# An attention-and-gating kernel in a fixed order of instructions: the order searched anew with more slack behind its transfers

## The chip, the cores and the metric

The kernel runs on one core of a Trainium2 chip. The metric is the device time of one execution in microseconds (us), lower being better. The core has five engines that run side by side and wait for each other by semaphores only: TensorE (PE, matrix products and transposes), VectorE (DVE), ScalarE (ACT), GpSimd (POOL) and SyncE (SP, which issues transfers). Sixteen DMA engines move data between the memory outside and the two memories on the core: SBUF, and PSUM, into which TensorE writes.

## The reference: chunk-selecting attention, then a gated layer

```python
# attention: q, k, v of shape (4, 8, 768, 64); chunks of 32 keys, 24 of them, 6 kept for each query
k_min = np.min(k_chunks, axis=3)
k_max = np.max(k_chunks, axis=3)
ub = np.sum(np.maximum(q[:, :, :, None, :] * k_min[:, :, None, :, :],
                       q[:, :, :, None, :] * k_max[:, :, None, :, :]), axis=-1)
ub = np.where(causal, ub, -1000000000.0)
top_chunks = np.argsort(ub, axis=-1)[..., -top_k:]
scores = scale * np.matmul(q, k.transpose(0, 1, 3, 2))
...                                           # mask: in a selected chunk, and not in the future
attn = np.exp(scores - np.max(scores, axis=-1, keepdims=True))
attn = attn / (np.sum(attn, axis=-1, keepdims=True) + 1e-09)
x = np.matmul(attn, v)                        # heads side by side: (4, 768, 512)

# gated layer
h = np.maximum(x @ w_in, 0.0)
u, v = (h[..., :d_ff // 2], h[..., d_ff // 2:])
v_n = (v - mu) / np.sqrt(var + 1e-06)         # over the last axis
v_s = np.einsum('ts,bsd->btd', w_spatial, v_n) + b_spatial[None, :, None]
return ((u * v_s) @ w_out).astype(np.float32)
```

## The kernel before

The work is cut into about 1,400 small operations with names. A pair `i` (0 to 15) is two heads of a batch; a batch `b` has four pairs; a group `g` is two pairs, loaded together. The number behind a name is the pair, or the batch and the tile of 128 rows. Names that matter here:

- `lk`, `lq`, `lv`: loads of keys, queries and values, issued by GpSimd; `win`, `wsp`, `wout`, `lb`: loads of the weights.
- `kT`, `kTb`, `qT`: transposes on TensorE; `kmax`, `kmin`, `kb`: bounds of the chunks on VectorE; `ub`: the upper bounds on TensorE; `top`, `sel`: the selection on VectorE; `kop`: copy of the transposed keys into the operand of the scores; `kh`: filling of that operand's constant half; `rq`: the positive and negative parts of the queries.
- `aT`, `ac`: transposes of the query operand and the copy out of PSUM, for pairs 0 to 7; `aTd`: the same as one transposing transfer of SyncE, for pairs 8 to 15.
- `sc`, `ex`, `av`: scores, exponentials, and the product with the values; `tri`: the causal triangle on GpSimd, from pair 4 on; `rc`, `nm`: normalisation on VectorE.
- `x`: transposition of the attention's output (by SyncE from pair 4 to pair 14); `v`, `u`, `s`, `o`: the four matrix products of the gated layer in pieces of two matmuls; `gt`: the gate; `gd`: transposition of the gate (SyncE, but for the last two, which go over TensorE, `gp`, and a copy, `gd`); `oc`, `os`: copy and store of the output.
- `dm`: matmuls on zeros that keep TensorE's clock up before there is work; `ring`, `small`, `expand`, `mlat`, `mtri`: constants.

A table says of each operation which engine has it, what it waits for and which buffers it takes. Each row also has an assumed duration. A search outside the kernel puts the operations into one list by means of these assumptions, and that list is what the kernel emits:

```python
DEF=dict(...,sc=3,tr=1,acc=1,ml=3,...,tm=.8,lm=0.2,lm2=1.2,...)
...
# loads of pair groups 1 to 7: (service time, assumed flight time)
op(f'lk{g}{hi}','POOL',1.007,...,dma=(p['svk'],1.9+(p['lm'] if g<4 else p['lm2'])))
...
# SyncE's transposing transfers: tm is the slack behind each
op(f'aTd{i}','SP',1.44,deps=[f'sel{i}'],acq=[('a',i)],uses=[('qs',g)],prio=pr(20),dma=(2.46,1.5+p['tm']))
...
op(f'x{i}','SP',1.22,deps=[f'nm{i}0',f'nm{i}1'],acq=[('xT',b)],uses=[('x16',i)],prio=t0+18,dma=(1.23,1.5+p['tm']))
...
else: op(f'gd{b}{ti}','SP',1.22,deps=[f'gt{b}{ti}'],acq=[('gT',f'{b}{ti}')],uses=[('g',f'{b}{ti}')],...,dma=(.82,1.5+p['tm']))
...
for n in p['flip']:                     # copies that go to the other of ScalarE and VectorE
    e,oc=o.alts; ...; o.eng,o.occ=e,oc
...
for k in range(p['dum']): op(f'dm{k}','PE',mmc(128),...)
```

```python
PLAN = {..., 'dum': 50, ..., 'flip': [...], 'lm': 0.2, 'lm2': 1.2, 'tm': 0.8, ...}
ORDER = """
dz id0 dm small lk000 ring2 ring1 lk010 ring0 lq000 ring3 id1 lq010 expand lk011 kh01 kh00 kh31 lk001 kT0 kh11 lq011
...
"""
...
with tc.manual_schedule():
    for name in ORDER.split():
        acts[name]()
```

Each engine runs its own operations in the order of the list, one after the other. The assumed durations are used nowhere else: they set no wait in the kernel. The buffers concerned: two for `x16` (the normalised output that `x` reads), three for `g`, one PSUM bank for `acc`, three for `sc`, three for the gated layer, and six for the output.

```python
def normalise(self, hi):                                    # nm
    if not hasattr(self, "x16"):
        self.x16 = sb.tile([P, NQT, 2, D], F16, tag="x16", name="x16")      # the pool has 2
    nc.vector.tensor_tensor(self.x16[:, :, hi, :], in0=self.av[hi][:, :, 0:D], ...)

def x_dma(self):                                            # x
    nc.sync.dma_start_transpose(out=self.x_dest()..., in_=self.x16.rearrange("p t h d -> p (t h d)"))

def gate():                                                 # gt
    g = st["g", ti] = ml.tile([P, DH], F16, tag="g", name="g", bufs=3)
    nc.vector.scalar_tensor_tensor(g, in0=st["s", ti], scalar=b_col[:, ti:ti + 1], in1=st["u"][:, ti, :], ...)

def gate_dma():                                             # gd
    st["gT", ti] = ml.tile([P, KO, P], F16, tag="gT", name="gT", bufs=NQT)
    if (b, ti) in prm["gp"]:
        copier(engine[f"gd{b}{ti}"])(st["gT", ti], st["gp", ti])
        return
    nc.sync.dma_start_transpose(out=st["gT", ti], in_=st["g", ti])

def scores(self, hi, g):                                    # sc
    sc = self.sc[hi, g] = ps_sc.tile([P, 512], F32, tag="sc", name="sc")
    for si, (t, q0, n, col) in enumerate(TILES[g]):
        diag = self.b == 0 and si == 0
        mm(sc[:, col:col + n], lhsT=self.kh[hi][:, t * P:(t + 1) * P], rhs=self.a[:, ...], start=True, stop=not diag)
        if diag:
            mm(sc[:, 0:P], lhsT=identity, rhs=tri, start=False, stop=True)
```

Of the kernel before, what the change touches and what calls it, by code (L numbers as in the profile page):

```python
# [166 lines left out]
def mmc(n): return max(n/2.4+2.5,25)/1000  # L167
DEF=dict(BEATS=12,pa=8,dve_a=(),qx=('ACT',),xp=4,mlp_first=13,mlp_mul=1.0,sc=3,tr=1,acc=1,ml=3,kbuf=3,qbuf=3,vbuf=3,ebuf=3,late=240,chunk=2,
  lk=40,lq=36,lv=18,kdma=99,kcp=2,kcdma=1,kc_act=(),shift=4,prep=0.0,tm=.8,lm=0.2,lm2=1.2,gp=(),head=1,lag=0.0,kp=27,ca=99,tree=0,svk=1.48,rpool=(),ract=(),svh=.96,svw=1.15,flip=(),wide=0,pt=(),kdm=0,xd=(),dum=0,dum0=42,split=1,warm0=0.,qa_dve=(),ma_act=(),mkbuf=2)
PEL=0.2  # L170
def build(prm=None):
    p=dict(DEF); p.update(prm or {})
# [17 lines left out]
    f=0.9  # L190
# [5 lines left out]
    for g in range(1,8):  # L196
        t0=2*g*BE
# [13 lines left out]
    for i in range(NPAIR):  # L211
        b,hp=divmod(i,HP); g,x=divmod(i,2)
        t0=i*BE
# [39 lines left out]
        ca=i>=p['ca']  # L253
# [36 lines left out]
        for hi in range(2):  # L290
            for gg in range(6):
                c=sum(mmc(n) for (_,_,n,_) in TILES[gg])+(mmc(128) if b==0 else 0)
                W_=p['wide']; kk=f'{i}{hi}{gg//2 if W_ else gg}'
                op(f'sc{i}{hi}{gg}','PE',c,PEL,deps=(adep[hi] if not hd else [f'acA0{hi}']+(['acB0'] if gg else []))+[f'kop{i}{hi}',f'kh{i%4}{hi}']+(['mtri'] if b==0 else []),acq=[('sc',kk)],uses=[('a',i),('kh',i)],prio=t0+6*hi+gg)
                if W_ and gg%2==0: continue
                op(f'ex{i}{hi}{gg//2 if W_ else gg}','ACT',(.493 if gg<5 else .16) if not W_ else (.915 if gg<5 else .60),.104,deps=[f'sc{i}{hi}{gg}']+([f'sc{i}{hi}{gg-1}'] if W_ else []),acq=[('e',f'{i}{hi}')],uses=[('sc',kk)],prio=t0+6*hi+gg+.1)
            EX=(lambda r: [f'ex{i}{hi}{gg}' for gg in sorted({x//2 for x in r})]) if p['wide'] else (lambda r: [f'ex{i}{hi}{gg}' for gg in r])
            tri=[]
            if b>0:
                op(f'tri{i}{hi}','POOL',.82,.05,deps=EX(range(6)),uses=[('e',f'{i}{hi}')],prio=t0+6*hi+6); tri=[f'tri{i}{hi}']  # L300
# [90 lines left out]
PLAN = {'late': 40, 'mlp_first': 8, 'qbuf': 5, 'kbuf': 6, 'vbuf': 6, 'dum': 50, 'warm0': 5.3, 'kcp': 99, 'flip': ['ac11', 'ac20', 'ac31', 'ac40', 'ac41', 'ac51', 'ac70', 'ac71', 'kc10', 'kc11', 'kc8', 'kc9', 'kh01', 'kh21', 'kh31', 'kop100', 'kop101', 'kop110', 'kop111', 'kop120', 'kop141', 'kop150', 'kop31', 'kop40', 'kop50', 'kop51', 'kop71', 'kop81', 'kop90', 'kop91', 'oc10', 'oc11', 'oc12', 'oc13', 'oc14', 'oc15'], 'gp': ((3, 4), (3, 5)), 'lm': 0.2, 'lm2': 1.2, 'tm': 0.8, 'dum0': 42, 'split': 1, 'rpool': (4,), 'ract': (1,)}  # L391

ORDER = """
dz id0 dm small lk000 ring2 ring1 lk010 ring0 lq000 ring3 id1 lq010 expand lk011 kh01 kh00 kh31 lk001 kT0 kh11 lq011
dm0 kTb0 kh30 kmin0 dm1 dm2 dm3 dm4 dm5 dm6 lq001 dm7 dm8 dm9 dm10 dm11 kop00 kmax0 qTb0 mlat qT0 dm12 lk10 dm13 rq01
dm14 dm15 dm16 rq00 dm17 dm18 dm19 dm20 dm21 dm22 dm23 kb0 kop01 ub0 lk11 kT1 top00 kTb1 kmin1 lv0 dm24 dm25 dm26 dm27
dm28 kop11 dm29 dm30 dm31 dm32 dm33 dm34 dm35 dm36 dm37 selA0 dm38 kmax1 kop10 aTA00 aTA01 mtri dm39 dm40 dm41 kh10
acA00 qT1 lq10 top01 sc000 kb1 dm42 dm43 sel0 dm44 ex000 rq11 aTB0 lq11 dm45 rq10 kh20 dm46 dm47 dm48 dm49 acB0 ub1
acA01 lb sc001 top10 sc005 kT2 ex001 sc002 win00 top11 ex005 sc004 sel1 ex002 win30 sc013 kmax2 aT10 ex004 lk21 sc010
ex013 sc003 kop21 ex010 lq20 sc011 kop20 aT11 ex003 av000 ex011 kmin2 sc015 lk20 av001 sc012 ac10 av002 ac11 lq21  # L400
ex015 sc100 ex012 rc00 kb2 sc014 kh21 ex100 nm00 qT2 lv1 qT3 ex014 rq21 sc102 sc112 rq20 ex102 kT3 rq30 sc101 win21
ex112 av010 kmin3 ub2 win10 ex101 sc104 sc111 win01 top20 ex104 av011 sc103 kmax3 av012 ex111 sc114 win31 ex103 sc113
top21 ex114 rc01 sc110 kb3 sel2 ex113 sc105 rq31 aT21 lk30 ex110 nm01 aT20 ex105 sc115 kop30 ac21 av100 ub3 ac20 av101
ex115 lk31 kop31 av102 top30 sc200 sc201 rc10 top31 ex200 kT4 nm10 sc205 ex201 win11 sc203 sel3 av110 ex205 kmin4
ex203 sc202 sc204 ex202 qT4 kmax4 av111 ex204 sc215 sc210 av112 ex215 aT30 rq41 ex210 sc213 rc11 rq40 kop40 sc211 wsp5
sc212 kb4 nm11 xp0 lq31 ex213 ub4 kop41 av200 ac30 av201 top40 win20 aT31 ex211 x0 av202 kT5 lq30 ex212 top41 sc214
kop50 sc300 rc20 sel4 sc301 lv2 nm20 qT5 ex214 ac31 av210 ex300 xp1 rq51 sc310 ex301 rq50 wsp0 av211 sc311 kmin5 ex310
aT40 sc303 ex311 av212 kmax5 sc304 ex303 wsp1 sc302 kT6 ex304 rc21 wout3 ac40 sc312 ex302 sc315 nm21 aT41 ex312 x1
sc305 av300 ex315 wsp3 ex305 sc313 kb5 kop51 ac41 sc404 sc314 kmin6 av301 ex313 ub5 av302 ex404 wsp4 top50 sc415 xp2
ex314 rc30 sc401 lk40 top51 ex415 nm30 sc402 ex401 sc403 sel5 ex402 av310 kop60 sc400 ex403 sc405 kT7 lk41 kmax6 ex405  # L410
aT50 ex400 av311 sc412 ac50 av312 kop61 ring4 sc411 ex412 rc31 sc501 x2 qT6 ex411 sc414 nm31 ex501 tri40 sc502 rq61
xp3 ex414 rq60 sc413 av400 wsp2 ex502 kmax7 aT51 ex413 lq40 sc410 sc500 x3 kop71 sc504 kb6 av401 ac51 v00.0 lq41 ex410
av402 kop70 ub6 ex500 sc513 kmin7 v00.2 ex504 lk51 sc503 ex513 sc512 kb7 v04.0 ex503 top60 lv3 v02.0 va00 top61 sc510
rc40 v04.2 sel6 ex510 nm40 sc514 lq50 qT7 ex512 v02.2 rq70 va04 av410 rq71 tri41 v03.0 va02 bs00 sc505 av411 ex514
aT60 bs04 sc511 ex505 av412 ac60 v03.2 lk50 rc41 bs02 v01.0 ex511 sc603 nm41 va03 ub7 tri50 v01.2 ex603 top70 x4 wsT0
lv4 va01 vs00 av500 top71 wsT1 wsc0 sc601 av501 sel7 sc600 ex601 lq51 bs03 sc602 v05.0 ex600 vs02 sc515 aT61 vs04 wsc1
ex602 wout1 sc605 v05.2 bs01 ac61 av502 u00.0 rc50 va05 vs01 u01.0 vs03 nm50 ex515 sc613 ex605 bs05 aT70 tri51 ex613
sc610 kT8 ac70 ex610 sc612 vs05 av510 kmin8 ex612 sc611 u00.2 ex611 kmax8 av511 sc615 qT8 ua00 sc704 av512 ex615 rq81
sc604 u01.2 ex704 rq80 sc703 ex604 rc51 kb8 aT71 nm51 sc700 ex703 sc614 tri60 ac71 av600 rs0 sc702 kop80 av601 ua01
ub8 av602 vn04 ex700 wsT2 rc60 ex614 nm60 sc701 wsT4 ex702 top80 tri61 av610 ex701 sc713 top81 sc712 kop81 av611 lk60  # L420
sel8 sc711 av612 wsc2 qT9 aTd8 ex713 rc61 wsT3 wsc4 wout0 u02.0 ex711 vn02 lv7 sc705 u04.0 ex712 vn00 x5 u02.2 ex705
wsc3 u04.2 ua02 nm61 tri70 sc710 wsT5 ua04 vn01 u03.0 ex710 wsc5 av700 sc715 rq90 sc714 u03.2 vn03 ex714 u05.0 vn05
ex715 kT9 ua03 tri71 u05.2 kmin9 s00.0 ua05 av701 s00.2 kmax9 s01.0 s00.4 rq91 kop90 s01.2 kb9 gt00 ub9 kop91 s01.4
top90 gd00 av702 sc801 top91 sc802 sc805 ex801 s02.0 rc70 sel9 kT10 ex802 gt01 aTd9 sc800 ex805 s02.2 nm70 ex800 sc810
sc815 kmin10 s02.4 ex810 x6 av710 ex815 qT10 kmax10 sc803 av711 sc804 ex803 av712 gt02 s03.0 gd01 ex804 sc814 rc71
kop100 s03.2 nm71 tri80 sc812 kb10 kT11 rq100 x7 kop101 s03.4 wout2 rq101 sc811 ex812 lq60 av800 gt03 ub10 gd02 kop111
s05.0 top100 s04.0 lq61 ex814 top101 s05.2 kmin11 ex811 av801 lq71 sc901 sc813 s05.4 ex901 sel10 sc903 kmax11 ex813
lk61 aTd10 qT11 s04.2 ex903 av802 kop110 sc911 lv5 sc904 rc80 sc914 nm80 s04.4 ex911 gt05 o00.0 ex914 lk70 sc902 kb11
av810 rq110 ex904 v10.0 ex902 tri81 sc913 o00.2 gt04 ex913 sc900 av811 oc00 rq111 sc915 v10.2 gd04 o02.0 va10 av812
sc905 o01.0 ex915 gd03 rc81 ex900 ub11 ex905 v11.0 top110 tri90 o02.2 bs10 v11.2 oc02 o01.2 top111 va11 sc910 v13.0  # L430
oc01 bs11 sc1000 v13.2 sel11 v12.0 nm81 va13 v14.0 ex910 qT12 bs13 kT12 ex1000 v14.2 kmax12 v12.2 va14 av900 vs13
sc912 va12 kop121 sc1002 av901 ex912 aTd11 sc1003 vs10 o03.0 kmin12 ex1002 tri91 sc1012 av902 ex1003 o03.2 rc90 x8
ex1012 lv6 v15.0 nm90 kop120 sc1005 kb12 sc1010 bs14 v15.2 av910 ex1005 bs12 ex1010 lq70 u10.0 gd05 oc03 sc1013 rq121
sc1001 av911 vs11 va15 rq120 lk71 u10.2 ex1013 sc1004 bs15 av912 ex1001 u11.0 rc91 sc1015 nm91 ua10 ub12 sc1014 vs14
ex1004 u11.2 top120 x9 o04.0 top121 ua11 tri100 kT13 vs15 sel12 ex1014 o04.2 kmin13 sc1011 ex1015 av1000 ex1011 sc1104
aTd12 kmax13 av1001 qT13 ex1104 sc1101 tri101 av1002 vs12 sc1112 ex1101 rq130 sc1114 u12.0 rc100 oc04 nm100 sc1102 rs1
u12.2 kop131 ex1112 av1010 o05.0 vn14 ex1114 av1011 kop130 sc1110 ex1102 o05.2 rq131 ua12 sc1100 av1012 kb13 ex1110
# [653 lines left out]
```

The softmax here doesn't subtract the row's maximum and nothing guards it: scores larger than these inputs give would overflow.

## Time and profile before

| what | value |
|---|---|
| time, median of three | 204.93 us (204.6 to 205.82) |
| span of the profiled execution | 202.8 us |
| TensorE, VectorE, ScalarE, GpSimd busy | 191.7, 158.9, 152.7, 80.9 us |
| granted TensorE clock | 1.00 |
| SyncE's transposes, median from issue to landing | gate 2.7, x 3.2, query operand 4.4 us |
| GpSimd's loads of k, q, v, median from issue to landing | 7.6, 7.1, 7.9 us |

A line of a group or of the chain names the engine, the line of the kernel and the tile written; L956 is every matmul of the gated layer, L832 the scores, L858 the product with the values, L868 `nm`, L999 `gt`, L877 `x`, L825 `aTd`, L1014 `gd`. A wait is put down to what came last before it ended. In the chain, a DMA piece runs from the issue to the landing.

### The profile page before, as it was taken

What the parts mean: (1) busy time and instruction counts of PE and PEld (TensorE: products, weight loads), DVE (VectorE), ACT (ScalarE), POOL (GpSimd) and SP (SyncE); (2) the same over time, 40 slices, a digit from 0 to 9 for tenths busy, and PEclk for the clock granted to TensorE, in tenths of its full rate; (3) what the DMA queues carried; (4) which work ended last, traced back from release to release, by engine and by line L of the source; (5) the groups of instructions that cost most, each with busy time, mean ns of one, the idle gap of its engine ahead of it and who ended that gap; (6) DMA issues with size and microseconds to landing.
All of it is one profiled execution on the core that took longest, in us unless ns stands there. A gap on an engine that the chain in (4) does not pass through costs nothing.

```text
span 202.8 us, 5261 instructions
## 1 busy us (share of the span) xinstructions
PE 191.7 (95%) x2043; PEld 121.0 (60%) x2043; DVE 158.9 (78%) x480; ACT 152.7 (75%) x299; POOL 80.9 (40%) x97
## 2 busy tenths in 40 slices
PE   7899899999999999999989999999999999999992
PEld 7776677876677755565456665556556555444441
DVE  6899799999899999796679999797677555367440
ACT  5979799999989976799589986594989542663141
POOL 7999858848871461196145211110113101000000
PEclk9999999999999999999999999999999999999999
DMA  6999999999999099989999958479181349150365
GB/s 39 108 119 165 157 179 170 161 198 133 150 142 157 1 106 116 207 99 151 149 129 181 157 143 157 123 167 181 39 214 61 91 102 122 26 209 0 81 248 192
DMA packets 113482, 27.02 MB, mean 133 GB/s; under 512 B 108465, under 2 KB 110001, under 8 KB 113457
## 3 DMA queue, kind: packets, MB, share of 16 engines
q0 software_dynamic: 76544, 12.20, 83.2%
q1 hardware_dynamic: 36912, 14.49, 36.6%
q8 instruction: 16, 0.26, 0.5%
q14 instruction: 10, 0.07, 0.1%
HBM read 24.38 MB, written 6.29 MB: 151 GB/s over the span
## 4 chain that ended last, share of the span: by engine, by line
PE 56%; DMA 17%; ACT 11%; POOL 6%; DVE 6%; issue 2%; SPq 1%; DVEq 0%; POOLq 0%
PE mlp L956 34%; PE sc L832 11%; ACT e L841 9%; DMA gT<-g 8%; PE acc L858 6%; DMA xT<-x 5%; DMA qs<-in_q_dram 4%; POOL k L618 2%; DVE g L999 1%; ACT kh L739 1%; POOL qs L618 1%; PE trq L744 1%; ACT a L822 1%; PE ub L764 1%; PE kTp L679 1%
## 5 line engine op out<-in xcount | busy, mean ns | idle before, releaser
L841 ACT ACTIVATE e<-sc 128x512 f16<-128x512 f32 (+1 forms) x192 | 92.9, 561 | 14.5 <-PE sc L832 10.9
L832 PE MATMUL sc<-a,kh 128*128 128x512 f16 (+3 forms) x256 | 61.8, 305 | 1.9 <-ACT a L822 0.5
L847 POOL TENSOR_SCALAR_AFFINE_SELECT e<-e 128x768 f16<-128x768 f16 x24 | 21.1, 877 | 80.8 <-ACT e L841 57.1
L956 PE MATMUL mlp<-w_in_sb,xT 128*128 128x512 f16 x192 | 51.9, 378 | 0.0
L858 PEld LDWEIGHTS <-e 128*128 128x128 f16 x672 | 31.5, 97 | 13.8 <-DVE x L868 0.9
L956 PE MATMUL mlp<-vn,wsT 128*128 128x512 f16 x144 | 38.3, 379 | 0.0
L858 PE MATMUL acc<-vt,e 128*128 128x65 f16 x672 | 35.9, 193 | 0.4 <-DVE x L868 0.4
L832 PEld LDWEIGHTS <-kh 128*128 128x128 f16 x256 | 22.6, 97 | 13.7 <-issue 0.7
L703 DVE TENSOR_REDUCE kmm<-kTp 128x24 f16<-128x768 f16 x32 | 29.8, 950 | 1.0 <-PE kTp L679 0.8
L956 PE MATMUL mlp<-w_out_sb,gT 128*128 128x512 f16 x92 | 26.7, 379 | 0.8 <-DMA gT<-g 0.5
L999 DVE SCALAR_TENSOR_TENSOR g<-mlp,b_col,u 128x512 f16<-128x512 f32 x24 | 18.0, 748 | 11.1 <-PE mlp L956 8.6
L956 PEld LDWEIGHTS <-xT 128*128 128x128 f16 x192 | 17.0, 97 | 14.5 <-issue 0.8
L978 DVE BATCH_NORM_STATS2 stats<-vraw 128x6 f32<-128x512 f32 x24 | 16.1, 684 | 9.0 <-ACT vraw L973 9.0
L988 ACT ACTIVATE u<-mlp 128x512 f16<-128x512 f32 x24 | 14.2, 599 | 9.1 <-PE mlp L956 8.4
L1019 ACT COPY o<-mlp 128x512 f32<-128x512 f32 x17 | 9.9, 585 | 13.5 <-PE mlp L956 13.4
L956 PEld LDWEIGHTS <-wsT 128*128 128x128 f16 x144 | 12.6, 97 | 10.7
L868 DVE TENSOR_TENSOR x<-acc,rec 128x384 f16<-128x384 f32 x32 | 17.6, 551 | 1.4 <-DMA xT<-x 1.0
L973 ACT ACTIVATE vraw<-mlp 128x512 f32<-128x512 f32 x24 | 14.0, 610 | 4.4 <-PE mlp L956 4.4
L774 DVE MAX8 max<-ub 128x8 f32<-128x8 f32 (+4 forms) x160 | 15.3, 165 | 1.6 <-PE ub L764 1.3
L603 POOL DMA_DIRECT2D k<-in_k_dram x14 | 14.7, 1047 | 1.5 <-DMA qs<-in_q_dram 1.1
L993 DVE TENSOR_SCALAR vn<-vraw,mv,rstd 128x512 f16<-128x512 f32 x24 | 13.7, 605 | 1.3 <-ACT rstd L1029 1.3
L609 POOL DMA_DIRECT2D qs<-in_q_dram x14 | 14.5, 1042 | 0.2 <-issue 0.2
(81 smaller groups left out, 238.0 us busy)
## 6 DMA issues: line engine op xcount, KB each, us to landing
out_dram<-o SPq DMA_DIRECT2D x23, 256.0 KB, 2.4
vt<-in_v_dram POOLq DMA_DIRECT2D x8, 384.0 KB, 7.9
k<-in_k_dram POOLq DMA_DIRECT2D x14, 192.0 KB, 7.6
qs<-in_q_dram POOLq DMA_DIRECT2D x14, 192.0 KB, 7.1
ws_raw<-in_moe_w_spatial_dram POOLq DMA_DIRECT2D x6, 192.0 KB, 7.8
w_in_sb<-in_moe_w_in_dram POOLq DMA_DIRECT2D x8, 128.0 KB, 7.9
w_out_sb<-in_moe_w_out_dram POOLq DMA_DIRECT2D x4, 128.0 KB, 6.9
k<-in_k_dram POOLq DMA_DIRECT2D x4, 96.0 KB, 3.4
```

The source lines that it names most:

```text
L603: nc.gpsimd.dma_start(out=k_tile(g)[:, :, :, hi, :].rearrange("p x t d -> p (x t) d"), in_=source(k, b, 2 * hp + 2 * hi, 2))
L609: nc.gpsimd.dma_start(out=t.rearrange("p x t d -> p (x t) d"), in_=source(q, b, 2 * hp + 2 * hi, 2))
L703: nc.vector.tensor_reduce(self.kmm[:, m, :], src, axis=AX.X, op=op, negate=(m == 1))
L774: nc.vector.max(self.max8[:, qi - 1, hi, :], self.ub[:, c0:c0 + CPT * (qi + 1)])
L832: mm(sc[:, col:col + n], lhsT=self.kh[hi][:, t * P:(t + 1) * P], rhs=self.a[:, q0 // P:(q0 + n) // P, hi, :], start=True, stop=not diag)
L841: nc.scalar.activation(out=self.e[hi][:, g * 512:g * 512 + width], in_=self.sc[hi, g][:, 0:width], func=Act.Exp, scale=scale)
L847: nc.gpsimd.affine_select(out=blk, in_=blk, compare_op=Alu.is_ge, fill=0.0, base=0, channel_multiplier=-1, pattern=[[0, NQT], [1, P]])
L858: mm(self.av[hi][:, qi, :], lhsT=self.e[hi][:, c:c + P], rhs=self.v[hi][:, t, 0:D + 1], start=first and n == 0, stop=last and n == len(blo ...
L868: nc.vector.tensor_tensor(self.x16[:, :, hi, :], in0=self.av[hi][:, :, 0:D], in1=self.rec[hi].to_broadcast([P, NQT, D]), op=Alu.mult)
L956: mm(st[kind, ti], lhsT=lhsT, rhs=rhs, start=(j == 0), stop=(j == n - 1))
L978: nc.vector.bn_stats(st["stats", ti], st["vraw"][:, ti, :])
L999: nc.vector.scalar_tensor_tensor(g, in0=st["s", ti], scalar=b_col[:, ti:ti + 1], in1=st["u"][:, ti, :], op0=Alu.add, op1=Alu.mult)
```

## The change

Two of the search's assumptions are larger: the slack behind each SyncE transpose, `tm`, goes from 0.8 to 1.6 us, and the slack behind the loads of groups 1 to 3, `lm`, from 0.2 to 0.6 us. It is meant to keep consumers from being listed so close behind a transfer that they wait for it when it lands late. The list of all operations was then searched anew. Seven more zero matmuls are in it (`dum` 50 to 57), and the set of copies that are swapped between ScalarE and VectorE differs. The condition of the diagonal matmuls is written with a parameter that has the same effect.

```diff
-PLAN = {'late': 40, 'mlp_first': 8, 'qbuf': 5, 'kbuf': 6, 'vbuf': 6, 'dum': 50, ..., 'flip': ['ac11', 'ac20', 'ac31', 'ac40', 'ac41', 'ac51', 'ac70', 'ac71', 'kc10', 'kc11', 'kc8', 'kc9', 'kh01', 'kh21', 'kh31', 'kop100', 'kop101', 'kop110', 'kop111', 'kop120', 'kop141', 'kop150', 'kop31', 'kop40', 'kop50', 'kop51', 'kop71', 'kop81', 'kop90', 'kop91', 'oc10', 'oc11', 'oc12', 'oc13', 'oc14', 'oc15'], ..., 'lm': 0.2, 'lm2': 1.2, 'tm': 0.8, ...}
+PLAN = {'late': 40, 'mlp_first': 8, 'qbuf': 5, 'kbuf': 6, 'vbuf': 6, 'dum': 57, ..., 'flip': ['ac10', 'ac11', 'ac21', 'ac31', 'ac40', 'ac41', 'ac51', 'ac60', 'ac71', 'gd34', 'gd35', 'kc10', 'kc11', 'kc8', 'kc9', 'kh00', 'kh01', 'kh31', 'kop100', 'kop101', 'kop111', 'kop140', 'kop141', 'kop150', 'kop31', 'kop40', 'kop50', 'kop51', 'kop71', 'kop81', 'kop90', 'kop91', 'oc05', 'oc10', 'oc12', 'oc14', 'oc15'], ..., 'lm': 0.6, 'lm2': 1.2, 'tm': 1.6, ...}
 ORDER = """
-dz id0 dm small lk000 ring2 ring1 lk010 ring0 lq000 ring3 id1 lq010 expand lk011 kh01 kh00 kh31 lk001 kT0 kh11 lq011
+dz id0 dm ring2 lk000 small lk010 ring3 lq000 id1 lq010 expand lk011 ring0 kh10 lk001 kh00 kT0 kh21 kh01 kh31 lq011
 ... (the whole list; the same names but for dm50 to dm56)
-                diag = self.b == 0 and si == 0
+                diag = self.i < prm["trip"] and si == 0        # trip = 4
```

The order of SyncE's transfers from pair 8's query operand to the gates of batch 0, and of GpSimd's loads in that stretch:

```
SyncE before   x4 aTd8 x5 gd00 aTd9 x6 gd01 x7 gd02 aTd10 gd04 gd03 aTd11 x8 gd05 x9 aTd12 x10
SyncE after    x4 aTd8 x5 x6 gd00 aTd9 gd01 gd02 x7 aTd10 gd03 x8 gd04 aTd11 gd05 aTd12 x9
GpSimd before  lv4 lq51 wout1 lk60 wout0 lv7 wout2 lq60 lq61 lq71 lk61 lv5 lk70 lv6 lq70 lk71
GpSimd after   lq51 lk60 lk50 lv4 lq50 lv7 wout0 wout2 lk61 lq61 lq60 lk71 lv5 lk70 lq70 lq71 lv6
```

## The prediction

> **What bounds the kernel now.** I read the page first (busy shares, then the 40 slices), then the busy times by stretch, then TensorE's waits, then the chain that ended last, and at the end the transfers one by one. The first view is part 1 of the page:
>
> ```profile
> span 202.8 us, 5261 instructions
> PE 191.7 (95%) x2043; PEld 121.0 (60%) x2043; DVE 158.9 (78%) x480; ACT 152.7 (75%) x299; POOL 80.9 (40%) x97
> ```
>
> TensorE is busy for 95% of the span. That share flatters it, so I did not stop there: a 512-column matmul is listed with 379 ns, but the chain below has pairs of them in 0.43 us, so the next one starts after 0.216 us. In the same way six transposes take 0.34 us (0.056 each) and nine value matmuls 0.28 us (0.031 each). I took the time from each matmul's start to the next one's start and subtracted this step. What is left over 40 ns is a true hole. The steps add up to 182.5 us and the holes to 14.7 us; the rest is the lead-in of 1.1 us and the tail after the last matmul. By stretch the holes are 10.8 us before 50 us, 0.5 us from 50 to 70, 2.8 us from 70 to 110, and 0.6 us from 110 to the end. The busy times by stretch (columns: PE, weight loads, DVE, ACT, POOL, each with its count, then clock, DMA share, GB/s) show the stages behind this:
>
> ```profile
> 0.00:50.00 50.00, 44.87 (x664) 36.27 (x665) 45.87 (x157) 44.56 (x82) 40.49 (x55) 1.00 1.77 143
> 50.00:70.00 20.00, 19.99 (x272) 13.97 (x270) 18.79 (x69) 19.00 (x41) 10.93 (x12) 1.00 1.75 118
> 70.00:112.00 42.00, 40.22 (x409) 23.82 (x408) 35.51 (x111) 34.41 (x67) 19.99 (x21) 1.00 1.59 139
> 112.00:165.00 53.00, 53.00 (x521) 30.82 (x519) 41.29 (x112) 39.21 (x82) 8.63 (x10) 1.00 0.68 131
> 165.00:202.80 37.80, 33.56 (x189) 16.07 (x185) 17.45 (x35) 15.55 (x31) 0.86 (x1) 1.00 0.46 124
> ```
>
> To 50 us no engine is full: loads, VectorE and ScalarE share the bound. From 50 us TensorE is full, and its only holes are waits. From 112 to 165 us there is nothing to win at all. The waits of TensorE and the DMA pieces of the chain (start, length, what) say which holes are the transfers':
>
> ```profile
> PE trq L744 <- DMA qs<-in_q_dram: 1.0, 1, 1.0
> PE mlp L956 <- DMA gT<-g: 0.5, 1, 0.5
> PE acc L858 <- DVE x L868: 0.4, 1, 0.4
> PE sc L832 <- DMA a<-qs: 0.4, 1, 0.4
> ```
>
> ```profile
> 14.11 7.15 DMA qs<-in_q_dram
> ...
> 72.70 10.05 DMA xT<-x
> ...
> 96.60 7.85 DMA gT<-g
> ...
> 165.85 4.41 DMA gT<-g
> ...
> 188.19 4.38 DMA gT<-g
> ```
>
> The third wait is a transfer in disguise: VectorE's L868 writes the x tile that the xT transfer of 72.70 us still reads, and TensorE needs the accumulator that L868 frees. So the later transfers cost five holes: 0.61 us at 82.6 (x5), 0.58 at 98.9 (aTd10), 0.69 at 103.8 (gd03), 0.33 at 170.6 (gd22) and 0.30 at 193.0 (gd31). Together that is 2.5 us, and it is all that slack behind SyncE transfers can return. The query load's hole at 20.1 us is 1.14 us.
>
> **What the skill says.** The Trainium skill, "Perfetto Trace Analysis", section Identifying the Most-Contended Engine, warns that TensorE's matmul busy share is no good measure because matmuls are pipelined; the 379 ns against steps of 216 ns agree, and it is why I count starts. "DMA: Bandwidth & Descriptors", section Issuing engines are not separate DMA queues, says that transfers from SyncE and GpSimd run on the same 16 DMA engines and interleave. The trace agrees: by each issue's time to landing, the twelve transposes issued between 81 and 111 us, with GpSimd loads in flight, land after 2.4 to 9.5 us, and those after 117 us after 2.3 to 4.4 us. "TensorE: Matmul & The Clock Gate", section What's actually happening, says that the array starts at half clock until it has been busy a while. The first 38 warm-up matmuls take 4.23 us here, 0.111 us each, and later ones 0.056, so this agrees; the granted clock is 1.00 in every stretch.
>
> **The change, part by part.** The arithmetic is the same. The renamed condition `i < trip` with 4 is the old `b == 0`, since four pairs make a batch: zero cost. Three things are left.
>
> (a) Seven more warm-up matmuls, 7 x 0.056 = 0.39 us of TensorE. They stand in holes before the first score, where TensorE waits for VectorE: no cost beyond what those waits already are.
>
> (b) Fifteen copies change between ScalarE and VectorE, so "engines as they were" is not exact. In the first 70 us VectorE gains kh00, ac10, ac21 and ac60, and gives up kh21, ac20 and ac70. Copies cost 0.51 (kh) and 0.55 us (ac) there, so the net is about +0.55 us, and ScalarE's is about -0.84 us (rows of L822, 836 ns). But kh00 falls early: VectorE runs without a break from the expansion at 4.35 us to the first bounds at 6.34 us, so these start about 0.3 to 0.5 us later, and with them the first selections. On ScalarE the zeroing of ring 1 (1.47 us) leaves the idle time at 2.1 us and comes after two kh copies, and kh20 now precedes the first exponential. By sum, the first exponential goes from 13.4 to about 14.5 us. That hardly counts, because the second one, at 15.0 us, waits for the second scores: those come near 15.3 us. Then comes the hole at 20 us. The loads lq10 and lq11 are issued back to back by GpSimd after the same work as before, so they still land at 21.2 us, and the query transposes cannot start sooner. However the new order puts more work before them: in listed TensorE work 14.05 against 13.39 us, less the 0.39 of warm-ups, so 0.27 us of useful work moves in. ScalarE too has a copy less and one more exponential there, in the 1.1 us that it idled before 22.4 us. So the head is about 0.3 worse at 15 us and about 0.3 better at 22 us: I put it at zero. From 22 to 70 us VectorE is the fullest engine together with ScalarE, and its own sum is nearly the same.
>
> (c) The order of transfers and consumers. For each transfer I added up the TensorE work (at the steps above) that the order list has between its issue and the first instruction that needs it, or needs the buffer it frees, and compared that with the landing time in this trace. Before and after, in us: x5 to the L868 that frees on it 9.15 and 8.16, with 10.05 needed; aTd10 to its scores 8.61 and 9.68, with 9.50 needed; gd03 to its output matmul 6.74 and 12.47, with 7.85 needed; gd22 to the gate that reuses its buffer 4.73 and 5.38, with 4.41 plus the gate's 0.75 needed; gd31 3.89 and 3.89, with 4.38 plus 0.75 needed. The three with more distance should lose their holes: 0.58 + 0.69 + 0.33 = 1.60, of which I count 1.2. For x5 the distance shrinks, but its landing should too: the loads issued beside it before (lk60, wout0 and lv7 at 70.3 to 73.3 us) now stand elsewhere, lk60 13 us of work sooner and wout0 10 us later; I count 0.4 of its 0.61. gd31 keeps its hole. Sum: -1.6 us.
>
> What may come new: aTd12's distance falls from 10.45 to 7.00 us, right beside lq71 and lv6, and it took 6.53 here; gd04's falls from 13.79 to 8.35 with 8.05 needed; x10's before its buffer is reused from 19.39 to 8.58. Each is above its need by 0.3 us or more, but issue times slip. In the tail gd34 and gd35 move from VectorE (0.425 us) to ScalarE (about 0.59), into gaps of 0.5 us between output copies. For all these I allow +0.6 us. Net: 0.0 - 1.6 + 0.6 = -1.0 us, so 204.9 - 1.0 = 203.9 us.
>
> **Rivals.** First, the slack takes the whole 2.5 us away and the head gains 1 us because loads are awaited where they really land: 201.4 us. For it speaks the distance table; against it that gd31 is unchanged and VectorE is full to 70 us. Second, the order simply trades waits: every distance was moved, 12.2 of the 14.7 us of holes have other causes than late SyncE transfers, and a new order on five in-order queues makes its own. SyncE then blocks behind one late transpose (x6 now stands ahead of gd00 and aTd9), and the loads still collide near 80 to 110 us: 206 to 207.5 us. For it speaks that the old order was tuned too; against it that most distances in that stage grew. Third, the later start of the scores is not caught up, as VectorE has no room to 70 us: +0.5 us, 205.4 us.
>
> **Range and chances.** TensorE's own steps leave little: to be faster by 2% (4.1 us) more than all five transfer holes would have to go and 1.6 us of the head besides. Slower by 2% needs holes of 4 us more, which one badly placed wait does not make, but several could. Range 201.6 to 207.0 us; faster by over 2% 0.06, within 2% 0.87, slower by over 2% 0.07.
>
> **What would show it.** Right: the holes at 98.9 and 103.8 us gone, 1.5 us or less of transfer holes after 70 us, 10 to 11.5 us of holes before 50 us, first exponential near 14.5 us and the second near 15.3. Wrong: TensorE's wait for `a<-qs` or `gT<-g` growing (step c), holes before 50 us over 12 us (step b), or a new wait in the stretch of 112 to 165 us, which had none.

## The result and the profile after

The changed kernel takes 201.98 us (201.74 to 202.01, four runs), against 204.76 us of the kernel before in the same runs: ratio 0.9854, 95% interval 0.9815 to 0.9894. In a second measurement the same kernel stood at 202.45 against 203.65 us: 0.9944, interval 0.9919 to 0.9968. So the gain is 1.2 to 2.8 us by the medians; the prediction had 1.0 and 203.9 us. I come back to the two measurements below. First the page of the changed kernel, part 1:

```profile
span 200.0 us, 5276 instructions
PE 190.3 (95%) x2050; PEld 121.0 (61%) x2050; DVE 159.8 (80%) x479; ACT 153.4 (77%) x300; POOL 81.6 (41%) x97
```

The busy share of TensorE is 95% as before and says nothing. The busy times by stretch say a little more (columns as before: PE, weight loads, DVE, ACT, POOL, clock, DMA share, GB/s):

```profile
0.00:50.00 50.00, 45.78 (x681) 36.89 (x682) 46.60 (x159) 44.98 (x82) 40.81 (x55) 1.00 1.77 145
50.00:70.00 20.00, 20.00 (x284) 14.39 (x283) 19.27 (x72) 19.11 (x41) 11.12 (x11) 1.00 1.82 114
70.00:112.00 42.00, 40.39 (x416) 24.45 (x414) 38.92 (x114) 35.09 (x71) 20.19 (x21) 1.00 1.65 139
112.00:165.00 53.00, 53.00 (x516) 30.65 (x514) 39.72 (x107) 39.52 (x81) 9.44 (x11) 1.00 0.76 137
165.00:200.00 35.00, 31.14 (x167) 14.66 (x162) 15.27 (x31) 14.68 (x28) 0.00 (x0) 0.98 0.42 126
```

From 70 to 112 us there are seven more matmuls, and yet PE is idle for 1.6 us. The waits of TensorE in that stretch name what is gone and what is new. The kernel before, then the changed one (us in total, times, longest):

```profile
PE mlp L956 <- DMA gT<-g: 0.5, 1, 0.5
PE acc L858 <- DVE x L868: 0.4, 1, 0.4
PE sc L832 <- DMA a<-qs: 0.4, 1, 0.4
PE wtr L648 <- DVE wsT L650: 0.4, 1, 0.4
```

```profile
PE kTp L680 <- DVE wsT L651: 1.6, 1, 1.6
```

(Line numbers behind the list of operations are one higher in the changed kernel, whose list is a line longer.) All three transfer waits are gone. One long wait on VectorE has come. Counted by start to start, as in the prediction, the holes of TensorE are, before and after: to 50 us 10.82 and 9.49; 50 to 70 us 0.48 and 0.08; 70 to 110 us 2.75 and 1.77; from there on 0.63 and 0.26. The sum falls by 3.07 us. The seven warm-ups add 0.39 us of steps, and the last matmul starts 2.69 us earlier, which agrees.

The transfers did not become faster. Time from issue to landing (min, median, max) of the gates, the x tiles and the query operands, in the changed kernel:

```profile
DMA to landing us min/median/max: 2.3/2.4/9.1
DMA to landing us min/median/max: 2.7/4.5/8.2
DMA to landing us min/median/max: 3.7/5.5/9.6
```

Before, the maxima were 8.1, 10.1 and 9.5 us, so two of three are longer now, that of the query operands by only 0.1 us, and two of three medians too (3.2 and 4.4 before). What changed is that nothing waits there.

The new hole is at 74.2 us and 1.77 us long. The first two blocks are VectorE and GpSimd of the changed kernel around it, the third is TensorE (start, length, engine, line, operation; in brackets the idle time before it):

```profile
71.58 3.91 DVE L994 TENSOR_SCALAR vn<-vraw,mv,rstd 128x512 f16<-128x512 f32 x4
75.42 0.54 DVE L651 COPY wsT<-wtr 128x768 f16<-128x768 f16 x1
75.88 0.99 DVE L994 TENSOR_SCALAR vn<-vraw,mv,rstd 128x512 f16<-128x512 f32 x2
```

```profile
71.67 1.17 POOL L848 TENSOR_SCALAR_AFFINE_SELECT e<-e 128x768 f16<-128x768 f16 x1 [2.79 <-ACT e L842]
72.80 1.03 POOL L610 DMA_DIRECT2D qs<-in_q_dram  x1
73.82 1.43 POOL L615 DMA_DIRECT2D vt<-in_v_dram  x1
```

```profile
74.06 0.34 PE L859 MATMUL acc<-vt,e 128*128 128x65 f16 x6
...
76.01 0.49 PE L680 MATMUL kTp<-identity,k 128*128 128x128 f16 x6 [1.61 <-DVE wsT L651]
```

Two normalisations take 0.99 us at 75.88, but four take 3.91 us at 71.58. While GpSimd is busy without a break, each of the last three takes 1.0 to 1.5 us and ends 0.22 to 0.28 us after a GpSimd instruction ends. The copy of the transposed weights (wsc) stands behind them and frees a PSUM bank late, and TensorE stands still for it. The experiments test this.

### The profile page after: what moved, and what is told of

It reads as the page before. It is cut to its first block, busy times and chain, and to the rows that moved or that the text cites. A ratio compares the mean times of both kernels' runs of the same rounds, so it can differ in the third digit from the quotient of the medians.

```text
span 200.0 us, 5276 instructions
## 1 busy us (share of the span) xinstructions
PE 190.3 (95%) x2050; PEld 121.0 (61%) x2050; DVE 159.8 (80%) x479; ACT 153.4 (77%) x300; POOL 81.6 (41%) x97
## 4 chain that ended last, share of the span: by engine, by line
PE 74%; DVE 8%; ACT 7%; POOL 4%; DMA 3%; issue 2%; POOLq 0%; DVEq 0%; ACTq 0%
PE mlp L957 45%; PE sc L833 13%; PE acc L859 8%; ACT e L842 6%; DMA vt<-in_v_dram 3%; DVE vn L994 2%; POOL k L619 2%; PE kTp L680 2%; PE ub L765 1%; PE tra L820 1%; POOL qs L619 1%; DVE kmm L704 1%; PE trq L745 1%; DVE wsT L651 1%; DVE max L775 1%
## 5 line engine op out<-in xcount | busy, mean ns | idle before, releaser
L833 PE MATMUL sc<-a,kh 128*128 128x512 f16 (+3 forms) x256 | 61.1, 305 | 1.2 <-ACT e L842 0.6
L848 POOL TENSOR_SCALAR_AFFINE_SELECT e<-e 128x768 f16<-128x768 f16 x24 | 21.6, 901 | 77.8 <-ACT e L842 73.3
L957 PE MATMUL mlp<-w_in_sb,xT 128*128 128x512 f16 x192 | 53.0, 379 | 0.0
L957 PE MATMUL mlp<-w_out_sb,gT 128*128 128x512 f16 x92 | 26.2, 379 | 0.0
L957 PEld LDWEIGHTS <-xT 128*128 128x128 f16 x192 | 16.5, 97 | 12.4 <-issue 0.2
L957 PEld LDWEIGHTS <-wsT 128*128 128x128 f16 x144 | 13.1, 97 | 12.4 <-issue 0.5
L1020 ACT COPY o<-mlp 128x512 f32<-128x512 f32 x18 | 10.6, 590 | 10.5 <-PE mlp L957 10.4
L994 DVE TENSOR_SCALAR vn<-vraw,mv,rstd 128x512 f16<-128x512 f32 x24 | 14.9, 674 | 2.1 <-ACT rstd L1030 2.1
L610 POOL DMA_DIRECT2D qs<-in_q_dram x14 | 14.5, 1036 | 0.4 <-issue 0.4
```

The costliest lines, as they stand in the source:

```text
L848: nc.gpsimd.affine_select(out=blk, in_=blk, compare_op=Alu.is_ge, fill=0.0, base=0, channel_multiplier=-1, pattern=[[0, NQT], [1, P]])
L957: mm(st[kind, ti], lhsT=lhsT, rhs=rhs, start=(j == 0), stop=(j == n - 1))
L994: nc.vector.tensor_scalar(vn[:, ti, :], in0=st["vraw"][:, ti, :], scalar1=st["mv"][:, ti, 0:1], scalar2=st["rstd"][:, ti, :], op0=Alu.subt ...
```

## The experiments

Intervals are those of the ratio to the kernel before; n is given where it is small. "v00.0" is the first matmul of the gated layer, at 50.19 us before and 49.00 us after in the two traces above.

### The changed order up to 49 us, the old one after it

Every operation ahead of v00.0 in the changed list comes in the changed order and on its engine; all others follow as before.

```diff
-ORDER = before
+ORDER = after[up to v00.0] + before[what is left]
```

> The changed order up to the first matmul of the gated layer (about 49 us), then every remaining operation in the order and on the engine of the kernel before. Theory (two separate gains: about 0.9 us in the head, where useful matmuls run in the hole before the query transposes, and about 1.8 us after it, where holes behind late transfers close): this kernel keeps the head's gain only, 0.7 to 1.2 us below the kernel before, and still has holes of TensorE between 80 and 105 us. Rival A (the head gain is swallowed by full VectorE later): within 0.3 us of the kernel before. Rival B (the whole gain comes from the head, and the stretch after only inherits it): 2.3 us or more below.

Measured: 203.68 us, ratio 0.9986 (0.996 to 1.0012). That is nearest to rival A, and less than the 0.7 us that I had as the least. In its trace v00.0 starts at 50.09 us, as late as before: the transposes of the second pair's keys waited 0.9 us for their load at 9.9 us, which they did not in the other traces with that head. From v00.0 to the last product it takes 148.19 us, before it took 148.07. The old waits are all back, and a longer one has joined them (TensorE from 70 to 112 us):

```profile
PE mlp L957 <- DVE g L1000: 1.3, 1, 1.3
PE wtr L649 <- DVE wsT L651: 0.4, 1, 0.4
PE acc L859 <- DVE x L869: 0.3, 1, 0.3
PE mlp L957 <- DMA gT<-g: 0.3, 1, 0.3
PE sc L833 <- DMA a<-qs: 0.2, 1, 0.2
```

The first line is the new one: the gate that frees the PSUM bank waits for a gate's transfer to land, VectorE for 2.46 us in front of it. So by itself the head gives little, 0.3 us by the ratio, and the interval includes no gain at all.

### The old order up to 50 us, the changed one after it

```diff
-ORDER = before
+ORDER = before[up to v00.0] + after[what is left]
```

> The order before up to the first matmul of the gated layer, then all remaining operations in the changed order and on its engines. Theory: keeps the gain after the head, 1.4 to 2.0 us below the kernel before, with the hole of 1.8 us near 75 us kept and those at 98.9 and 103.8 us gone; together with the other half it sums to about 2.7 us. Rival A (the head gain is nothing): 2.5 us or more below. Rival B: within 0.4 us of the kernel before.

Measured: 202.52 us, ratio 0.9921 (0.9892 to 0.995), 1.6 us less, as the theory had it. v00.0 to the last product takes 146.44 us; in the changed kernel 146.57. The hole at 74.7 us is 1.76 us long. The greater part of the gain is here.

### Two loads away from the normalisation

```diff
 GpSimd: ... tri60 tri61
-tri70 lq50 lv7 tri71 wout0 wout2 tri80
+lq50 tri70 tri71 wout0 wout2 lv7 tri80
```

> The changed kernel with two of GpSimd's loads moved in the list: lq50 ahead of tri70, lv7 behind wout2, so that GpSimd does not issue them while VectorE normalises (vn, 73 to 75.5 us). Theory (VectorE's vn takes 1.0 to 1.5 us in place of 0.54[...]; the wsc copy behind it is late, and TensorE waits 1.77 us for the bank): vn back to 0.54 to 0.6 us there, the hole of 1.77 us gone or under 0.4, time 1.2 to 1.8 us below the changed kernel. Rival (VectorE has too much work there whatever GpSimd does): hole over 1 us, time within 0.4 us of the changed kernel. A second rival: the load lq50, issued beside the transposes of 69 to 73 us, delays them, and a new hole eats the gain.

Measured: 202.49 us, ratio 0.9929 (0.9898 to 0.996), which is not better than the changed kernel's two ratios, 0.9854 and 0.9944 (it did not run beside this one). The mechanism held nevertheless: the last four of the six normalisations take 0.53 us each (the second, beside a triangle, still 1.08), and the hole is 0.30 us. But lv7, now issued at 81.8 us among the transposes, lands only after 10.7 us, gd01 and gd02 take 8.9 and 8.7 us, 7.0 and 5.8 in the changed kernel, and TensorE waits again from 70 to 112 us:

```profile
PE mlp L957 <- DVE g L1000: 0.8, 1, 0.8
PE sc L833 <- DMA a<-qs: 0.7, 1, 0.7
PE mlp L957 <- DMA xT<-x: 0.2, 1, 0.2
```

The second rival was right about the kind of loss. For the waits near 93 us the run with both loads early, further below, speaks for lv7 and not lq50: there they are gone. The wait for `a`, a hole of 0.84 us at 109.9 us, comes long after lv7 has landed at 92.5 us; in that later run TensorE also waits near 110 us, so lv7's place alone does not explain it.

### The old order with two consumers later

```diff
 TensorE: ... sc910 v13.0
-sc1000 v13.2 v12.0
+v13.2 v12.0 sc1000
 ... sc1003
-o03.0 sc1012 av902 o03.2 v15.0 sc1005 sc1010 v15.2
+sc1012 av902 v15.0 sc1005 sc1010 v15.2 o03.0 o03.2
 ScalarE:
-oc03 ... va15
+va15 oc03
```

> The kernel before with two consumers listed later, nothing else: the scores that read aTd10's operand behind one more pair of matmuls, and the output matmuls that read gd03 behind four more (its output copy behind va15). Theory (a hole behind a late transfer is lost TensorE time): the holes of 0.58 and 0.69 us at 98.9 and 103.8 us go, and 0.9 to 1.3 us of time with them. Rival (other engines are the bound there and the wait moves on): within 0.3 us of the kernel before, with new holes of the same sum by 112 us.

Measured: 203.09 us, ratio 0.9957 (0.993 to 0.9984), 0.9 us less: the theory's lower end. Both holes, 1.27 us, are gone; two new ones of 0.27 and 0.29 us have come. Of TensorE's waits from 70 to 112 us, its trace lists this one alone; the other holes are under 0.3 us each:

```profile
PE wtr L648 <- DVE wsT L650: 0.4, 1, 0.4
```

### The changed kernel once more

> The changed kernel, unaltered, beside the next three on one chip, as their yardstick. Expected: 2.0 to 3.0 us below the kernel before, the hole of about 1.8 us near 75 us again, no hole over 0.3 us from 80 us on, and the start of the first matmul of the gated layer at 49.0 to 49.6 us (loads' landing times differ by some tenths from run to run). If that start or the holes differ by more, single traces of the head decide nothing.

Measured: 202.45 us, ratio 0.9944 (0.9919 to 0.9968): 1.1 us less, below the 2.0 that I had as the least. The trace looks as expected: hole of 1.77 us at 74.4 us, nothing over 0.22 us after it, v00.0 at 49.20. What moved is the other side. The kernel before ranged from 202.5 to 205.5 us in 39 runs, the changed one from 201.8 to 203.2 in 12. The first measurement had four runs of each.

### lv7 near 125 us in the changed kernel

```diff
 GpSimd: ... tri60 tri61
-tri70 lq50 lv7 tri71 ... tri120
+lq50 tri70 tri71 ... tri120 lv7
```

> The changed kernel with lq50 ahead of tri70, as in the run that moved both loads, but lv7 (the values of the last group, first needed near 150 us) behind tri120, near 125 us, where no other load is in flight. Theory (in the first attempt the hole at 75 us closed, and lv7's 384 KB among the transposes of 80 to 95 us opened new ones): hole at 75 us under 0.4 us, no hole over 0.4 us from 80 to 112 us, time 1.2 to 1.7 us below the changed kernel. Rival (once TensorE runs 1.5 us ahead there, the transposes of that stretch are late for it whatever lv7 does): holes of 1 us or more between 88 and 112 us, time within 0.5 us of the changed kernel.

Measured: 202.70 us, ratio 0.9954 (0.9925 to 0.9983): no gain, against the theory. Its profile was taken in a disturbed execution, so I read no times from it, and whether lv7 held up the gates' transposes that this order has beside it stays open.

### lv7 near 125 us in the kernel before

```diff
 GpSimd: ... lk60 wout0
-lv7 tri70 ... tri120
+tri70 ... tri120 lv7
```

> The kernel before with lv7 behind tri120, nothing else. Theory (x5's transpose took 10 us because GpSimd's loads were issued beside it, lv7 the largest): x5 lands after 3 to 7 us, the hole of 0.5 to 0.6 us near 82.5 us goes, VectorE's vn of 1.4 us at 72 us falls to about 1.0 or less, and the time falls by 0.4 to 1.0 us. Rival (x5 is slow behind lk60 and wout0, or behind aTd8's transpose, whatever lv7 does): x5 still lands after 9 us or more, time within 0.3 us of the kernel before.

Measured: 202.60 us, ratio 0.9936 (0.9912 to 0.996), 1.3 us less, more than the theory had. x5 lands after 8.07 us, so neither the 3 to 7 us of the theory nor the rival's 9 us: without lv7 a fifth of its 10 us is gone, no more. Nor is this all gain: aTd8, issued just before x5, now lands after 9.32 us instead of 7.69, and TensorE has a new hole for its `a` operand, 0.60 us at 80.0 us. (In the four traces that have the old order there with lv7 late, x5 takes 7.3 to 8.1 and aTd8 8.6 to 9.3 us; in the three with lv7 in its place, 9.7 to 10.1 and 7.7 to 7.8.) The hole at 82.5 us is gone, and with it those at 98.9 and 103.8 us, which I had not expected. The slow normalisation of 1.40 us is gone too, with the hole of 0.55 us at 73.5 us behind it: the five from 72 us on take 0.53 to 0.65. So this one move acts in two ways, and no run separates them.

### Three moves in the old order

lv7 as in the last one, and the two consumers of the earlier one.

```diff
 the two edits above together
```

> The kernel before with lv7 last and with the two consumers listed later (aTd10's scores, gd03's output matmuls): three moves by hand in the old order. Theory (the change's gain after the head is the removal of these waits and nothing else): 1.4 to 2.0 us below the kernel before, as the half of the changed order after the head gave. Rival (the new order gains by something else there): 1.0 us or less below.

Measured: 201.72 us, ratio 0.9921 (0.9892 to 0.995), 1.6 us by the ratio of the runs and 1.9 by the medians. This is what the theory says, and as much as the whole new order gives. The list of TensorE's waits from 70 to 112 us is empty in this trace (largest hole 0.29 us), and the stretch is fuller than in any trace shown so far:

```profile
70.00:112.00 42.00, 41.86 (x433) 25.52 (x432) 37.47 (x113) 36.29 (x73) 18.53 (x20) 1.00 1.53 139
```

### The two loads earlier in the changed kernel

```diff
 GpSimd: ... tri51
-tri60 tri61 tri70 lq50 lv7 tri71
+lq50 lv7 tri60 tri61 tri70 tri71
```

> The changed kernel with lq50 and lv7 ahead of their place by three triangles, behind tri51 (about 63 to 66 us), where GpSimd is idle and no VectorE normalisation and no transpose of SyncE is under way. Theory (the hole of 1.77 us at 75 us is GpSimd's hold[...]; both earlier tries failed by where they put lv7, not by the cause): hole at 75 us under 0.4 us, holes from 80 to 112 us under 0.5 us in sum, time 1.0 to 1.7 us below the changed kernel (202.0 to 202.5 us): about 200.9 us. Rival (lv7 always delays the transposes that come next, here aTd8, x5 and x6 of 69 to 73 us): aTd8 lands after 9 us or more, a new hole of 0.5 us or more at 80 to 82 us, time within 0.7 us of the changed kernel.

Measured: 201.42 us (n = 6), ratio 0.9834 (0.9782 to 0.9885). The kernel of the next but one experiment, which differs from the changed one by unused matmuls alone, has 202.30 us on the same chip, so this is 0.9 us less: between theory and rival, with intervals that overlap (six runs each). VectorE in the stretch of the old hole (three normalisations, the first of them beside a triangle at 1.08 us and the others at 0.53, then two):

```profile
72.76 1.99 DVE L994 TENSOR_SCALAR vn<-vraw,mv,rstd 128x512 f16<-128x512 f32 x3
74.68 0.54 DVE L651 COPY wsT<-wtr 128x768 f16<-128x768 f16 x1
75.15 0.99 DVE L994 TENSOR_SCALAR vn<-vraw,mv,rstd 128x512 f16<-128x512 f32 x2
```

The copy comes 0.74 us sooner though this trace began the gated layer 0.73 us later (49.73), and the hole is 0.31 us. aTd8 and x5 land after 5.4 and 4.6 us, so the rival is wrong. A new wait takes part of the gain in the profiled run, which had 202.07 us:

```profile
111.63 0.61 PE L957 MATMUL mlp<-w_out_sb,gT 128*128 128x512 f16 x2 [0.90 <-DMA gT<-g]
```

This is gd05, issued at 103.8 and landed after 7.82 us. Its distance in the changed list is 8.46 us of TensorE work, and enough while TensorE is late and it lands after 5.61 us, as in the changed kernel's trace. The six runs fall in two groups, 200.62 to 200.78 and 202.07 to 202.43. That this wait divides them is likely but was not shown.

### The changed head before the three moves

```diff
-ORDER = before with the three moves
+ORDER = after[up to v00.0] + before with the three moves[what is left]
```

> The changed order up to the first matmul of the gated layer, then the order before with the three moves by hand (lv7 last, the two consumers later). Theory (the head's gain of about 0.5 us and the removed waits add up): 0.3 to 0.9 us below the three moves alone, about 201.1 us. Rival (the head gives nothing that survives): within 0.3 us of the three moves alone.

Measured: 201.68 us (n = 6), ratio 0.9859 (0.9807 to 0.9911). The three moves alone have 202.15 on that chip, 0.47 us more. It lies in the theory's range; the intervals overlap, so it is no proof.

### Seven warm-ups fewer

```diff
-PLAN = {..., 'dum': 57, ...}
+PLAN = {..., 'dum': 50, ...}
-dm48 dm49 dm50 dm51 dm52 acA00 dm53 dm54 kop11 dm55 dm56 rq11
+dm48 dm49 acA00 kop11 rq11
```

> The changed kernel with 50 single warm-up matmuls as before, dm50 to dm56 left out (they compute nothing that is used). Theory (they fill a hole that is there anyway): within 0.3 us of the changed kernel, first scores at the same time within 0.2 us. Rival (they stand in front of the first scores): 0.3 to 0.4 us below the changed kernel.

Measured: 202.30 us (n = 6), ratio 0.9873 (0.9828 to 0.9918). The first scores start at 13.94 us and the second at 14.84; with 57 warm-ups they start at 13.95 and 14.85. So they do not delay the scores, and no cost shows.

### The three moves once more

> The kernel before with the three moves by hand, unaltered, beside the other three on one chip. Expected: 1.4 to 2.3 us below the kernel before once more, no hole over 0.4 us from 75 to 112 us.

Measured: 202.15 us (n = 6), ratio 0.9895 (0.9836 to 0.9954), 2.1 us less by the ratio, no hole over 0.3 us from 75 to 112 us.

## Why the prediction came out as it did

**Transfers (step c): the mechanism right, the size too small.** I counted 1.6 of the 2.5 us of five holes. All five went, the whole 2.5 us. x5 landed after 4.47 us with the loads beside it moved, as argued. gd31's hole I had kept because its distance is the same 3.89, and it went too. But the two holes of the tail (gd22 and gd31), 0.63 us together, are no fixed cost of the old order: in six other traces with the old tail they come to 0.00 to 0.24 us. So the new order can be credited with about 1.9 us of the 2.5. The run with two consumers later shows that such holes are TensorE time: of the 1.27 us that it closes, 0.9 come through. The three moves give as much as the new order, so no other merit of the new order is needed after 50 us.

**New waits: the size wrong and the cause not foreseen.** I allowed 0.6 us, for aTd12, gd04, x10 and two copies of the tail. None of these made a hole. There are two others. One of 0.20 us at 185.9 us ends 0.05 us after a gate of VectorE does, so it is no transfer's. The 1.77 us at 74 us came from GpSimd issuing loads during VectorE's normalisation; the trace before had already the sign of it, one normalisation of 1404 ns among a median of 540, and a wait of 0.4 us for wsT. I read the group's mean, 605 ns, and not its maximum (before and after; minimum, median and maximum in ns):

```profile
L993 DVE TENSOR_SCALAR vn<-vraw,mv,rstd x24: 501/540/1404, 68.2 to 184.7; 128x512 f16<-128x512 f32 x24
L994 DVE TENSOR_SCALAR vn<-vraw,mv,rstd x24: 508/544/1520, 71.6 to 182.0; 128x512 f16<-128x512 f32 x24
```

Taking the loads away, in the two runs above, brings the normalisations that they stood beside back to 0.53 us and the hole to 0.3.

**Head (step b): the marks of the exponentials right, the sum not.** The first exponential was to come near 14.5 us and the second near 15.3; they came at 14.42 and 15.32. The holes before 50 us were to be 10 to 11.5 us; they are 9.49. Nor are all of these waits, as I had it: the first warm-ups start 0.106 us apart, where I subtracted 0.056, which makes 2.0 us of the holes before and 1.5 of those after. (The 0.111 us of the prediction is their busy time divided by their number.) I put the head's gain at zero. In the two traces it is 1.19 us at v00.0. But lq11 had landed 0.9 us sooner, at 20.36 against 21.26 us, and this lies within the scatter: over six traces of the old head it lands at 20.55 to 21.56 us, over seven of the new head at 20.36 to 21.39. By the start of v00.0 over the same traces, the old head has 49.48 to 50.49 us, mean 49.92, the new one 49.00 to 50.09, mean 49.40: 0.52 us, with ranges that overlap. The hole before the query transposes varies with the landing, and the new order has more work to put into it; the run with the head alone does not confirm more than this.

**Warm-ups (step a):** no cost that shows, as predicted.

**The sum.** Predicted: 0.0 head - 1.6 transfers + 0.6 new waits = -1.0 us. In the traces: -1.19 to v00.0; +0.94 from there to the first product with the spatial weights (27.77 us against 26.83), where the new hole lies; -2.44 from there to the end (118.80 against 121.24). That is -2.69 us. In the prediction's own terms: -1.2 head, -2.5 transfers, +2.0 new waits, and about -1.0 that I had no term for, the hole of 0.55 us at 73.5 us and several of 0.1 to 0.2. Of the head's part about half is likely to be chance. So it is partly luck that the second measurement, 1.1 us by its ratio, lies so near to my 1.0: in these traces the transfers were counted 0.9 us too small and the new waits 1.4 too small, and these errors work against each other. Of the rivals, the first (all the slack taken and the head faster, 201.4 us) came closest to the first measurement, but it had no new hole in it.

**What stays open.** Which of the two measurements is the better one. A third value, of the changed kernel with seven warm-ups fewer, lies between them, 0.9873. Beside the second measurement the kernel before varied by 3 us and the changed one by 1.4, and I did not show which waits do that; between the traces that have parts of the old order, the loads' landings and the waits of 80 to 105 us differ. What the head gives by itself is open too, and so is the wait near 110 us of the two runs in which the hole at 74 us was closed.

## What to carry to other kernels

On in-order queues a late transfer costs nothing until its consumer is listed too near, so compare, for each transfer, the work listed between issue and first need (the reuse of its source buffer included) with its longest landing, not the median. Such slack may hold for one pace only: both runs of the changed kernel above that mended the stall at 74 us had a new wait near 110 us, as if the engine that runs ahead ate the distance, though this cause was not tested. Before a new search, try the few moves that the waits name: three of them gave here what the search of 1,400 operations gave, and without its new hole.

## What the runs showed of the hardware

A VectorE operation on SBUF alone can be held up by GpSimd's issuing of a load, not only by its arithmetic. The normalisation (128 x 512, fp32 to fp16) takes 0.54 us. Beside GpSimd's issues of 1.03 and 1.43 us it took 1.01 and 1.52 us, and beside a triangle of 1.17 us 1.09 us, ending 0.22 to 0.28 us after GpSimd's instruction each time. The Trainium skill, "SBUF — State Buffer", section SBUF: two separate sides, says that VectorE in its two-port modes and GpSimd take one port pair by an exclusive lock, and that the one that starts first has it for its whole instruction. The trace agrees: what remains after GpSimd's end is nearly the same, 0.22 to 0.28 us, for its instructions of 1.03 to 1.43 us, and the normalisation that began 0.09 us before the triangle kept its 0.54 us. That the normalisation runs in such a mode, and that the port is what it waits for, no run here shows.
